# One ring for both caches of a decode attention, V in 64 KB rows, w_down on 64 partitions, all of wo last

## The chip, the cores and the metric

The kernel runs on one core of a Trainium2 chip. The metric is the device time of one execution in microseconds (us), the median of several runs. Five engines work side by side and are tied by semaphores: PE (matrix products), DVE (vector), ACT (activations), POOL, and SP, which here does nothing but issue the transfers (DMAs) from HBM to SBUF. SBUF has 128 partitions; PSUM is where PE accumulates.

## What is computed

Two branches of a decoding step for one token, mixed by a gate:

```python
q = (x @ wq).reshape(1, 1, 32, 128)               # x: 512, wq: 512 x 4096
scores = einsum("bhqd,bhkd->bhqk", q, k_cache) * 128 ** -0.5   # k_cache: 32 x 65536 x 128
o = einsum("bhqk,bhkd->bhqd", softmax(scores), v_cache)        # v_cache: 32 x 65536 x 128
a = o.reshape(1, 1, 4096) @ wo                    # wo: 4096 x 512
b = (silu(x @ w_gate) * (x @ w_up)) @ w_down      # 512 x 1792, 512 x 1792, 1792 x 512
g = sigmoid((x * gate_w).sum(-1))
out = g * a + (1 - g) * b
```

All is in bf16. The two caches are 537 MB each, and every byte of them is read once; all weights together are 14 MB.

## The kernel before

There are 32 heads of 65536 rows. A head is cut into G = 4 chunks of 16384 rows, so that K and V come in 128 chunks each, 4 MB a chunk: 128 rows of the cache (NB) in each of the 128 partitions, 32 KB in a row of HBM. A chunk n belongs to head n // 4.

For a chunk of K, `products` multiplies all rows by the head's query on DVE (line 228, one instruction in place) and halves the 128 products three times by additions (line 232); `scores` adds the remaining 16 columns up on PE with 16 products with the identity (line 242) into the head's 128x512 scores in PSUM. When a head's four chunks are in, `row_max` and `exponentials` take the largest score and write the weights P_sb; DVE does this between the halves of the next chunk's products. For a chunk of V, `values` issues 32 products of PE (line 290). At the end of a head, `head_copy` and `head_column` bring the four partial rows into a column oT (lines 303, 311, 318), and `project` multiplies it with the head's 128 rows of wo into a_ps (line 323). The feed-forward branch (`feed_forward_in`, `_mid`, `_out`) runs between the first chunks.

The schedule is manual: each engine does its instructions in the order in which the program writes them. Every transfer is issued by SP, in one queue, in the program's order, so a transfer whose place in SBUF is still in use holds up all that are issued after it. The large tiles come from one pool, `ring`, of SLOTS = 5 slots of 32 KB a partition: chunks of K, chunks of V, wq, w_gate with w_up, w_down and the second half of wo. A step of the main loop takes one chunk of K and one of V; V follows four chunks of K behind (up to eight later, `LAG` and `SPREAD`). The first half of wo comes in four pieces between the chunks into `wo_pool`, and the heads of that half are projected as they finish; the second half of wo is loaded after the last chunk of V, and its heads are projected at the end. Ahead of the main loop SP issues x, gate_w, wq, two chunks of K, w_gate, w_up, w_down and the first piece of wo.

The tile framework gives each transfer one of eight semaphores in turn, and adds a wait wherever an instruction touches bytes that an earlier one reads or writes, as far as it can tell from the two access patterns.

Of the kernel before, what the change touches and what calls it, by code (L numbers as in the profile page):

```python
# [11 lines left out]
P = 128  # L12
# [4 lines left out]
SLOTS = 5  # L17

WIDTH = 16

LAG = 8
SPREAD = 40
# [3 lines left out]
def kernel(  # L26
# [22 lines left out]
    FT = F // P  # L49
    G = Sk // (NB * P)  # L50
    NBH = Sk // P
    N = H * G
    QG = 4
    assert Dh == P and Sk % (NB * P) == 0 and NBH <= 512 and H % QG == 0 and G >= 2
# [3 lines left out]
    ring = ctx.enter_context(tc.tile_pool(name="ring", bufs=SLOTS))  # L58
    small = ctx.enter_context(tc.tile_pool(name="small", bufs=2))
    ppool = ctx.enter_context(tc.tile_pool(name="ppool", bufs=3))  # L60
    wo_pool = ctx.enter_context(tc.tile_pool(name="wo_pool", bufs=2))
# [7 lines left out]
    def big(name):  # L69
        return ring.tile([P, NB * Dh], bf16, name=name, tag="big")  # L70


    xT = consts.tile([P, KT], bf16, name="xT")
    gwT = consts.tile([P, KT], bf16, name="gwT")
    with nc.allow_non_contiguous_dma(reason="small"):
        nc.sync.dma_start(out=xT, in_=A_x[0, 0, :].rearrange("(p t) -> p t", t=KT))
        nc.sync.dma_start(out=gwT, in_=gate_w.rearrange("(p t) -> p t", t=KT))
    wq_t = big("wq_t")
    wq_sb = wq_t[:, : KT * H * Dh].rearrange("p (t f) -> p t f", t=KT)
    nc.sync.dma_start(out=wq_sb, in_=A_wq.rearrange("(p t) f -> p t f", t=KT))  # L80
# [9 lines left out]
    X_bc = consts.tile([P, KT, P], bf16, name="X_bc")  # L90
# [7 lines left out]
    b_sb = consts.tile([1, D], f32, name="b_sb")  # L98
    a_ps = psum_a.tile([1, D], f32, name="a_ps")

    K_tiles, V_tiles, S_tiles, P_tiles, O_tiles = {}, {}, {}, {}, {}

    def load(dst, cache, n, name, cuts=(0, NB)):
        h, g = divmod(n, G)
        t = big(name)
        view = t.rearrange("p (j d) -> p j d", d=Dh)
        src = cache[0, h, g * NB * P : (g + 1) * NB * P, :].rearrange("(p j) d -> p j d", j=NB)
        for a, b in zip(cuts[:-1], cuts[1:]):
            nc.sync.dma_start(out=view[:, a:b, :], in_=src[:, a:b, :])
        dst[n] = view  # L110

    load(K_tiles, A_k_cache, 0, "K_t")
    load(K_tiles, A_k_cache, 1, "K_t")

# [14 lines left out]
    for g in range(H // QG):  # L129
        queries(g)  # L130


    gu_t = big("gu_t")
    wgu_sb = gu_t[:, : 2 * KT * F].rearrange("p (w t f) -> p w t f", w=2, t=KT)
    nc.sync.dma_start(out=wgu_sb[:, 0], in_=B_w_gate.rearrange("(p t) f -> p t f", t=KT))
    nc.sync.dma_start(out=wgu_sb[:, 1], in_=B_w_up.rearrange("(p t) f -> p t f", t=KT))
    wd_t = big("wd_t")
    wd_sb = wd_t[:, : FT * D].rearrange("p (t n) -> p t n", t=FT)
    nc.sync.dma_start(out=wd_sb, in_=B_w_down.rearrange("(p t) n -> p t n", t=FT))
    WG = 4  # L140
    wo_tiles = {}

    WH = H // 2
    wo_end = []

    def load_wo_end(cuts):
        t = big("wo_t")[:, : (H - WH) * D].rearrange("p (h n) -> p h n", n=D)
        rows = A_wo[WH * P :, :].rearrange("(h p) n -> p h n", p=P)
        for a, b in zip(cuts[:-1], cuts[1:]):
            nc.sync.dma_start(out=t[:, a:b, :], in_=rows[:, a:b, :])  # L150
        wo_end.append(t)

    def load_wo(g):
        wo_tiles[g] = wo_pool.tile([P, WG, D], bf16, name="wo_sb")
        rows = A_wo[g * WG * P : (g + 1) * WG * P, :]
        nc.sync.dma_start(out=wo_tiles[g], in_=rows.rearrange("(h p) n -> p h n", p=P))

    load_wo(0)

    def feed_forward_in():  # L160

        gu_ps = psum_m.tile([P, 2 * FT], f32, name="gu_ps", tag="misc")
        for w in range(2):
            cols = wgu_sb[:, w].rearrange("p t (m c) -> p t c m", c=FT)
            for ft in range(FT):
                for t in range(KT):
                    nc.tensor.matmul(
                        gu_ps[:, w * FT + ft : w * FT + ft + 1],
                        lhsT=cols[:, t, ft, :],
                        rhs=xT[:, t : t + 1],  # L170
                        start=(t == 0),
                        stop=(t == KT - 1),
                    )
        gu_sb = consts.tile([P, 2 * FT], f32, name="gu_sb")
        nc.scalar.activation(out=gu_sb, in_=gu_ps, func=ACT.Copy)
        eg = consts.tile([P, FT], f32, name="eg")
        nc.scalar.activation(out=eg, in_=gu_sb[:, :FT], func=ACT.Exp, scale=-1.0)
        return gu_sb, eg

    def feed_forward_mid(gu_sb, eg):  # L180
# [10 lines left out]
        b_ps = psum_m.tile([1, D], f32, name="b_ps", tag="misc")  # L191
        for ft in range(FT):
            nc.tensor.matmul(  # L193
                b_ps,
                lhsT=hT[:, ft : ft + 1],
                rhs=wd_sb[:, ft, :],
                start=(ft == 0),
                stop=(ft == FT - 1),
            )
        g_ps = psum_m.tile([P, 1], f32, name="g_ps", tag="misc")  # L200
# [3 lines left out]
        return b_ps, eg2  # L204

    def feed_forward_out(b_ps, eg2):

# [5 lines left out]
        )  # L213
        nc.scalar.activation(out=b_sb, in_=b_ps, func=ACT.Copy, scale=rest)
        nc.tensor.matmul(a_ps, lhsT=ones_f[0:1, 0:1], rhs=b_sb, start=True, stop=False)  # L215


    def products(n, a=0, b=NB):

# [31 lines left out]
    def row_max(h):  # L251

        m = small.tile([P, 1], f32, name="m")
        nc.vector.tensor_reduce(out=m, in_=S_tiles[h], axis=AXIS.X, op=ALU.max)  # L254
        diag = small.tile([P, P], f32, name="diag")
# [17 lines left out]
    def total(h):  # L273

        tot_ps = psum_m.tile([P, 1], f32, name="tot_ps", tag="misc")
        nc.tensor.matmul(tot_ps, lhsT=ones_f, rhs=rowsum[:, h : h + 1], start=True, stop=True)  # L276
        return tot_ps
# [6 lines left out]
    def values(n):  # L284

        h, g = divmod(n, G)
        if g == 0:
            O_tiles[h] = psum_o.tile([4, 4 * Dh], f32, name="O_ps")
        for j in range(0, NB, 4):
            nc.tensor.matmul(  # L290
                O_tiles[h],
                lhsT=P_tiles[h][:, g * NB + j : g * NB + j + 4],
                rhs=V_tiles[n][:, j : j + 4, :],
                start=(g == 0 and j == 0),
                stop=(g == G - 1 and j == NB - 4),
            )
        del V_tiles[n]

    def head_copy(h, last=False):
        O_sb = small.tile([4, 4 * Dh], f32, name="O_sb")  # L300
# [21 lines left out]
    def project(h):  # L322
        nc.tensor.matmul(  # L323
            a_ps,
            lhsT=oT[:, h : h + 1],
            rhs=wo_tiles[h // WG][:, h % WG, :] if h < WH else wo_end[0][:, h - WH, :],
            start=False,
            stop=(h == H - 1),
        )


    steps = []
    v = 0
    for n in range(N):
        due = n >= G and not (n >= SPREAD and n % 4 == 3 and n - v < LAG)
        steps.append((n, v if due else None))
        v += due
    while v < N:
        steps.append((None, v))
        v += 1  # L340

    ff = done = tot_ps = None
    for n, v in steps:
        if n is not None and n > 1:
            load(K_tiles, A_k_cache, n, "K_t")
        if v is not None:
            if v % (WG * G) == 2 * G and v // (WG * G) + 1 < WH // WG:
                load_wo(v // (WG * G) + 1)
            load(V_tiles, A_v_cache, v, "V_t", (0, NB) if v < N - 2 else (0, 64, NB) if v < N - 1 else (0, 32, 64, 96, 112, NB))
            if v == N - 1:  # L350
                load_wo_end((0, 4, 8, 12, 14, 16))
        vector = iter(()) if n is None else products(n)
        top_of = None
        if n is None:
            top_of = H - 1 if S_tiles else None
        elif n % G == 0 and n > 0:
            top_of = n // G - 1
            vector = (i for a in (0, NB // 2) for i in products(n, a, a + NB // 2))
        if top_of is not None:
            next(vector, None)  # L360
            mT_ps = row_max(top_of)
            next(vector, None)
            exponentials(top_of, mT_ps)
        for _ in vector:
            pass
        if n == 1:
            ff = feed_forward_in()
        if n == 2:
            ff = feed_forward_mid(*ff)
        if n == 3:  # L370
            feed_forward_out(*ff)
        if tot_ps is not None:
            weight(*tot_ps)
            tot_ps = None
        if done is not None:
            head_column(done, head_copy(done))
        if v is not None:
            values(v)
        if top_of is not None:
            tot_ps = top_of, total(top_of)  # L380
        if n is not None:
            scores(n)
        if done is not None and done < WH:
            project(done)
        done = v // G if v is not None and v % G == G - 1 else None
    O_last = head_copy(H - 1, last=True)
    for h in range(WH, WH + 4):
        project(h)
    head_column(H - 1, O_last)
    for h in range(WH + 4, H):  # L390
        project(h)

    out_sb = consts.tile([1, D], bf16, name="out_sb")
# [32 lines left out]
```

## Time and profile before

| | |
|---|---|
| time, median of 3 runs | 2543.51 us (2541.84 to 2543.7) |
| profiled execution: time / span of the core | 2541.8 us / 2540.0 us |
| busy: PE / DVE / ACT | 1736.3 us (68%) / 2174.9 us (86%) / 75.7 us (3%) |
| read from HBM | 1087.64 MB, 428 GB/s over the span |
| mean clock granted to PE | 0.751 |

The profile's page is of one execution. "Busy" is the time in which an engine executes; the slices are 40 equal parts of the span, with a digit for tenths of busy time. The chain that ended last is followed back from the last instruction to what released it. The timeline lists instructions in the order of their start, with equal neighbours merged (xN), and in brackets the idle time before them and what ended it. A row with SPq is an issue of a transfer; the transfer itself lands later.

### The profile page before, as it was taken

The numbers are of one execution on the slowest core, as the hardware profiler recorded it, in microseconds if no ns is written. First come the engines' busy times: TensorE is split into PE (matmuls) and PEld (weight loads), VectorE is DVE, ScalarE is ACT, GpSimd is POOL, SyncE is SP. The second block draws the span as 40 slices with busy tenths as digits, with TensorE's granted clock in tenths as the row PEclk, the third lists the DMA queues.
The fourth block names the chain that finished last, engine by engine and source line by source line (L and its number), as shares of the span: only waits on it lengthen the run. The fifth ranks groups of instructions, "written<-read, shape, count | busy, mean of one in ns | idle before, by whom it ended". The sixth has DMA issues, their size and how long they took to land.

```text
span 2540.0 us, 15211 instructions
## 1 busy us (share of the span) xinstructions
PE 1736.3 (68%) x6722; PEld 707.9 (28%) x6722; DVE 2174.9 (86%) x780; ACT 75.7 (3%) x206; POOL 0.7 (0%) x6
## 2 busy tenths in 40 slices
PE   3577667776777656667776667677667776776679
PEld 2232222322223222222232223222222222222223
DVE  6999888888888999998888888888888888888860
ACT  1000000000000000000000000000000000000000
POOL 0000000000000000000000000000000000000000
PEclk7777776777777677777777777777777777777779
DMA  9999999999999999999999999999999999999998
GB/s 408 428 431 430 432 431 432 430 429 432 431 432 431 429 432 432 430 432 431 431 431 430 434 431 431 431 431 432 430 432 431 431 431 430 433 431 431 431 431 358
DMA packets 42755, 1088.61 MB, mean 429 GB/s; under 512 B 4673, under 2 KB 8770, under 8 KB 9026
## 3 DMA queue, kind: packets, MB, share of 16 engines
q1 hardware_dynamic: 42690, 1087.66, 99.7%
q8 instruction: 52, 0.85, 0.1%
q14 instruction: 13, 0.11, 0.0%
HBM read 1087.64 MB, written 0.00 MB: 428 GB/s over the span
## 4 chain that ended last, share of the span: by engine, by line
DMA 67%; PE 21%; DVE 11%; issue 1%; ACT 0%; SPq 0%; DVEq 0%
DMA V_t<-in_A_v_cache_dram 60%; PE O_ps L290 19%; DVE K_t L228 6%; DMA K_t<-in_A_k_cache_dram 5%; DVE K_t L232 5%; PE S_ps L242 1%; DMA wo_t<-in_A_wo_dram 1%; DMA wq_t<-in_A_wq_dram 0%; PE qg_ps L118 0%; PE oh_ps L311 0%; DVE m L254 0%; PE a_ps L323 0%; ACT P_sb L267 0%; PE a_ps L215 0%; DVE top L263 0%
## 5 line engine op out<-in xcount | busy, mean ns | idle before, releaser
L290 PE MATMUL O_ps<-V_t,P_sb 128*4 128x512 bf16 x4096 | 1159.0, 453 | 494.7 <-DMA V_t<-in_A_v_cache_dram 492.5
L228 DVE TENSOR_TENSOR K_t<-K_t,q_bc 128x16384 bf16<-128x16384 bf16 (+1 forms) x159 | 1117.2, 7026 | 267.5 <-DMA K_t<-in_A_k_cache_dram 259.1
L232 DVE TENSOR_TENSOR K_t<-K_t 128x2048 bf16<-128x2048 bf16 (+3 forms) x477 | 1030.5, 2160 | 14.2
L290 PEld LDWEIGHTS <-P_sb 128*4 128x4 bf16 x4096 | 394.2, 97 | 1240.9 <-issue 899.0
L242 PE MATMUL S_ps<-K_t,ident_b 128*128 128x128 bf16 x2048 | 464.4, 392 | 118.4 <-DVE K_t L232 118.4
L242 PEld LDWEIGHTS <-ident_b 128*128 128x128 bf16 x2048 | 225.6, 114 | 341.7 <-issue 148.3
L311 PE MATMUL oh_ps<-ident_f,O_sb 4*128 4x1 f32 x256 | 57.1, 340 | 73.7 <-ACT O_sb L303 73.7
L311 PEld LDWEIGHTS oh_ps<-ident_f,O_sb 4*128 4x128 f32 x256 | 54.4, 310 | 83.5 <-ACT O_sb L303 78.8
L256 ACT ACTIVATE diag<-ident_f,m 128x128 f32<-128x128 f32 x32 | 12.9, 402 | 2100.6 <-DVE m L254 2100.6
L258 PE MATMUL mT_ps<-diag,ones_f 128*128 128x128 f32 x64 | 24.0, 475 | 74.9 <-ACT diag L256 74.9
L305 DVE COPY O_sb<-O_ps 4x256 f32<-4x256 f32 x1 | 0.4, 412 | 52.7 <-ACT O_sb L303 52.7
L258 PEld LDWEIGHTS mT_ps<-diag,ones_f 128*128 128x128 f32 x64 | 14.9, 290 | 90.5 <-ACT diag L256 90.5
L254 DVE TENSOR_REDUCE m<-S_ps 128x1 f32<-128x512 f32 x32 | 21.9, 684 | 7.2 <-PE S_ps L242 7.2
L267 ACT ACTIVATE P_sb<-S_ps,bias 128x512 bf16<-128x512 f32 x32 | 22.0, 687 | 1.0
L303 ACT ACTIVATE O_sb<-O_ps 4x512 f32<-4x512 f32 (+1 forms) x32 | 18.1, 565 | 131.5 <-PE O_ps L290 131.5
L118 PE MATMUL qg_ps<-wq_t,X_bc 128*128 128x512 bf16 x32 | 9.6, 473 | 14.0 <-DMA wq_t<-in_A_wq_dram 14.0
L193 PE MATMUL b_ps<-wd_t,hT 128*1 128x512 bf16 x14 | 5.1, 545 | 15.7 <-DVE hT L186 15.7
L281 DVE RECIPROCAL recip<-tot_ps 128x1 f32<-128x1 f32 x32 | 5.1, 160 | 12.1 <-PE tot_ps L276 12.1
L276 PEld LDWEIGHTS tot_ps<-rowsum,ones_f 128*128 128x128 f32 x64 | 9.5, 188 | 14.0 <-issue 14.0
L276 PE MATMUL tot_ps<-rowsum,ones_f 128*128 128x1 f32 x64 | 12.2, 260 | 0.0
L318 ACT ACTIVATE oT<-oh_ps,rg 128x1 bf16<-128x1 f32 x32 | 8.4, 264 | 75.9 <-PE oh_ps L311 75.9
L263 DVE TENSOR_REDUCE top<-mT_ps 128x1 f32<-128x128 f32 x32 | 9.0, 283 | 1.2 <-PE mT_ps L258 1.2
(39 smaller groups left out, 64.6 us busy)
## 6 DMA issues: line engine op xcount, KB each, us to landing
K_t<-in_A_k_cache_dram SPq DMA_DIRECT2D x128, 4096.0 KB, 35.3
V_t<-in_A_v_cache_dram SPq DMA_DIRECT2D x126, 4096.0 KB, 29.5
wq_t<-in_A_wq_dram SPq DMA_DIRECT2D x1, 4096.0 KB, 12.3
V_t<-in_A_v_cache_dram SPq DMA_DIRECT2D x2, 2048.0 KB, 31.9
V_t<-in_A_v_cache_dram SPq DMA_DIRECT2D x3, 1024.0 KB, 31.1
wo_sb<-in_A_wo_dram SPq DMA_DIRECT2D x4, 512.0 KB, 36.9
gu_t<-in_B_w_gate_dram SPq DMA_DIRECT2D x1, 1792.0 KB, 34.6
gu_t<-in_B_w_up_dram SPq DMA_DIRECT2D x1, 1792.0 KB, 38.3
```

Of the source, the lines that this page charges most:

```text
L118: nc.tensor.matmul(qg_ps, lhsT=X_bc[:, t, :], rhs=wq_sb[:, t, g * QG * Dh : (g + 1) * QG * Dh], start=(t == 0), stop=(t == KT - 1),)
L228: yield nc.vector.tensor_tensor(out=K, in0=K, in1=q_rep, op=ALU.mult)
L232: yield nc.vector.tensor_tensor(out=K[:, :, 0:half], in0=K[:, :, 0:half], in1=K[:, :, half : 2 * half], op=ALU.add,)
L242: nc.tensor.matmul(S_tiles[h][:, g * NB : (g + 1) * NB], lhsT=ident_b, rhs=K_tiles[n][:, :, c], start=(c == 0), stop=(c == WIDTH - 1),)
L254: nc.vector.tensor_reduce(out=m, in_=S_tiles[h], axis=AXIS.X, op=ALU.max)
L256: nc.scalar.activation(out=diag, in_=ident_f, func=ACT.Copy, scale=m)
L258: nc.tensor.matmul(mT_ps, lhsT=ones_f, rhs=diag, start=True, stop=True)
L267: nc.scalar.activation(out=P_tiles[h], in_=S_tiles[h], func=ACT.Exp, bias=bias, scale=scale, accum_out=rowsum[:, h : h + 1],)
L276: nc.tensor.matmul(tot_ps, lhsT=ones_f, rhs=rowsum[:, h : h + 1], start=True, stop=True)
L290: nc.tensor.matmul(O_tiles[h], lhsT=P_tiles[h][:, g * NB + j : g * NB + j + 4], rhs=V_tiles[n][:, j : j + 4, :], start=(g == 0 and j == 0) ...
L303: nc.scalar.activation(out=O_sb[:, :cut], in_=O_ps[:, :cut], func=ACT.Copy)
L311: nc.tensor.matmul(oh_ps, lhsT=O_sb[:, c * Dh : (c + 1) * Dh], rhs=ident_f[0:4, c : c + 1], start=(c == 0), stop=(c == 3),)
```

## The change

All 192 KB of a partition that the ring takes are now one tensor of six units of 32 KB, and the program says which unit each load uses. Units 0 and 1, 2 and 3, 4 and 5 form pairs.

- K still comes in chunks of 4 MB, but the rows are dealt out so that a partition owns 256 rows of the cache in sequence (64 KB): a chunk of K reads the first or the second 32 KB of each such row. V comes in 64 loads of 8 MB, 64 KB a partition, into a pair of units (`load_v`); the last two of them are loaded in halves and smaller cuts.
- The main loop runs over pairs of K chunks: step j loads chunks 2j-1 and 2j into one pair of units and V load j-2 into the next, and uses V load j-2's first half in step j and its second in step j+1.
- w_down lies on 64 partitions, 28 rows of it in each (28 KB), in unit 4. It is loaded by eight transfers of eight partitions each, which are 4 partitions apart (`load_wd`): two before K chunk 2, two before chunk 3, two before chunk 4, two before the first V load. The hidden vector is brought into that layout by two products with columns of the identity (h_ps, h2), and its product with w_down takes 28 matmuls in place of 14, in `feed_forward_out`.
- SP's first load is the part of wq for heads 0 to 3, then x, K chunk 0, the rest of wq, gate_w, w_gate, w_up, K chunk 1. The products of K chunk 0 start after the first four heads' queries.
- wo is loaded whole after the last V, in seven cuts, and all 32 heads are projected at the end: 8 before the last head's column, 24 after.
- P_sb has two buffers instead of three; diag, O_sb and b_sb one.

The core of the diff:

```diff
-    ring = ctx.enter_context(tc.tile_pool(name="ring", bufs=SLOTS))
+    ring = consts.tile([P, UNITS * UNIT], bf16, name="ring")
+    def unit(u, size=UNIT, parts=P):
+        return ring[:parts, u * UNIT : u * UNIT + size]
+    def rows_of(cache, h, c):
+        rows = cache[0, h, c * 2 * NB * P : (c + 1) * 2 * NB * P, :]
+        return rows.rearrange("(p j) d -> p j d", j=2 * NB)
+    def load_k(n, u):
+        h, g = divmod(n, G)
+        view = unit(u).rearrange("p (j d) -> p j d", d=Dh)
+        half = g % 2
+        nc.sync.dma_start(
+            out=view, in_=rows_of(A_k_cache, h, g // 2)[:, half * NB : (half + 1) * NB, :]
+        )
+        K_tiles[n] = view
+    def load_v(w, pair):
+        h, c = divmod(w, 2)
+        view = ring[:, 2 * pair * UNIT : 2 * (pair + 1) * UNIT].rearrange("p (j d) -> p j d", d=Dh)
+        nc.sync.dma_start(out=view, in_=rows_of(A_v_cache, h, c))
...
+    nc.sync.dma_start(out=wq_sb[:, :, :first], in_=wq_rows[:, :, :first])
...
+    load_k(0, 1)
+    nc.sync.dma_start(out=wq_sb[:, :, first:], in_=wq_rows[:, :, first:])
...
+    wd_sb = unit(4, GT * D, HP).rearrange("p (t n) -> p t n", t=GT)
+    wd_rows = B_w_down.rearrange("(p t) n -> p t n", t=GT)
+    def load_wd(i):
+        lo = (0, 1, 2, 3, 32, 33, 34, 35)[i]
+        part = slice(lo, lo + 29, 4)
+        nc.sync.dma_start(out=wd_sb[part], in_=wd_rows[part])
...
-        for ft in range(FT):
-            nc.tensor.matmul(
-                b_ps,
-                lhsT=hT[:, ft : ft + 1],
-                rhs=wd_sb[:, ft, :],
...
+        h_ps = psum_m.tile([HP, GT], f32, name="h_ps", tag="misc")
+        for r in range(2):
+            nc.tensor.matmul(
+                h_ps[:, r * FT : (r + 1) * FT], lhsT=ident_b[:, r::2], rhs=hT, start=True, stop=True
+            )
+        h2 = consts.tile([HP, GT], bf16, name="h2")
+        nc.scalar.activation(out=h2, in_=h_ps, func=ACT.Copy)
...
+        for t in range(GT):
+            nc.tensor.matmul(
+                b_ps, lhsT=h2[:, t : t + 1], rhs=wd_sb[:, t, :], start=(t == 0), stop=(t == GT - 1)
+            )
...
+    queries(0)
+    drain(products(0))
+    for g in range(1, H // QG):
+        queries(g)
+    load_k(1, 3)
+    load_wd(0)
+    load_wd(1)
+    load_k(2, 5)
+    scores(0)
+    ff = feed_forward_in()
+    for j in range(1, last + 1):
+        a, b = 2 * j - 1, 2 * j
+        pair = 2 * (j - 2) % 3
+        if j == 2:
+            for i in range(3):
+                load_wd(2 + 2 * i)
+                load_wd(3 + 2 * i)
+                if i < 2:
+                    load_k(3 + i, i)
+        elif j > 2:
+            load_k(a, 2 * pair)
+            load_k(b, 2 * pair + 1)
+        if j == last:
+            load_k(NK - 1, 2 * ((pair + 1) % 3))
+        elif j >= 2:
+            load_v(j - 2, (pair + 1) % 3)
+        drain(products(a))
+        if j == 1:
+            ff = feed_forward_mid(*ff)
...
+        if j >= 3:
+            values(j - 3, 1)
...
+        if j == last:
+            load_v(j - 2, (pair + 2) % 3)
+        scores(a)
...
+        if b % G == 0:
+            sums = maximum(b // G - 1, (i for c in (0, NB // 2) for i in products(b, c, c + NB // 2)))
+        else:
+            drain(products(b))
...
+        if j == 2:
+            feed_forward_out(*ff)
+        if j >= 2:
+            values(j - 2, 0)
+        scores(b)
+    drain(products(NK - 1))
+    values(NV - 3, 1)
+    O_sb = head_copy(H - 2)
+    load_v_half(NV - 2, 0, 2 * pair)
+    load_v_half(NV - 2, 1, 2 * pair + 1)
+    load_v_half(NV - 1, 0, 2 * spare + 1, (0, 64, NB))
+    scores(NK - 1)
+    head_column(H - 2, O_sb)
+    weight(*maximum(H - 1, iter(())))
+    load_v_half(NV - 1, 1, 2 * spare, (0, 32, 64, 96, 112, NB))
...
+    cuts = (0, 8, 16, 22, 26, 29, 31, 32)
+    for lo, hi in zip(cuts[:-1], cuts[1:]):
+        nc.sync.dma_start(out=wo_sb[:, lo:hi, :], in_=wo_rows[:, lo:hi, :])
+    for w in (NV - 2, NV - 1):
+        for half in range(2):
+            values(w, half)
+    O_sb = head_copy(H - 1, last=True)
+    for h in range(8):
+        project(h)
+    head_column(H - 1, O_sb)
+    for h in range(8, H):
+        project(h)
```

## Prediction

> **What bounds the kernel now.** I read the slices first, then the chain, then the timeline at both ends.
>
> ```profile
> span 2540.0 us, 15211 instructions
> ...
> DVE  6999888888888999998888888888888888888860
> ...
> DMA  9999999999999999999999999999999999999998
> GB/s 408 428 431 430 432 431 432 430 429 432 431 432 431 429 432 432 430 432 431 431 431 430 434 431 431 431 431 432 430 432 431 431 431 430 433 431 431 431 431 358
> ...
> DMA 67%; PE 21%; DVE 11%; issue 1%; ACT 0%; SPq 0%; DVEq 0%
> ```
>
> The transfers are the bound: 431 GB/s from the second slice to the 39th, and no engine is full. Only the outer slices (63.5 us each) fall short, by (431-408)/431 x 63.5 = 3.4 us and (431-358)/431 x 63.5 = 10.8 us. At 431 GB/s a 4 MB chunk takes 9.73 us. So what matters is whether SP keeps the queue fed, and what is left to do when the last bytes land. The timeline of the start:
>
> ```profile
> 1.66 0.42 SPq L80 DMA_DIRECT2D wq_t<-in_A_wq_dram  x1
> 2.13 0.91 SPq L109 DMA_DIRECT2D K_t<-in_A_k_cache_dram  x2
> ...
> 57.20 3.63 PE L242 MATMUL S_ps<-K_t,ident_b 128*128 128x128 bf16 x16 [6.35 <-DVE K_t L232]
> 58.95 8.69 DVE L228 TENSOR_TENSOR K_t<-K_t,q_bc 128x16384 bf16<-128x16384 bf16 x1 [1.81 <-DMA K_t<-in_A_k_cache_dram]
> ...
> 67.68 8.01 DVE L232 TENSOR_TENSOR K_t<-K_t 128x8192 bf16<-128x8192 bf16 x3
> ```
>
> By 5.1 us SP has issued 18.6 MB, so DVE's 16.7 us a chunk (8.69 + 8.01) hides behind transfers. And the end:
>
> ```profile
> 2461.33 3.63 PE L242 MATMUL S_ps<-K_t,ident_b 128*128 128x128 bf16 x16
> ...
> 2466.24 0.64 PE L258 MATMUL mT_ps<-diag,ones_f 128*128 128x128 f32 x2 [1.29 <-ACT diag L256]
> ...
> 2468.78 1.86 PE L311 MATMUL oh_ps<-ident_f,O_sb 4*128 4x1 f32 x8 [1.90 <-ACT O_sb L303]
> ...
> 2470.57 8.38 PE L290 MATMUL O_ps<-V_t,P_sb 128*4 128x512 bf16 x32
> ...
> 2479.20 20.88 PE L290 MATMUL O_ps<-V_t,P_sb 128*4 128x512 bf16 x96
> ...
> 2534.19 2.94 PE L323 MATMUL a_ps<-wo_t,oT 128*1 128x512 bf16 x12
> ```
>
> A chunk of V costs PE 8.4 to 9.9 us after idling, 7.0 when it runs on (20.88/3); a projection 0.245. The last matmul ends at 2537.1, 2.9 us before the span.
>
> **The start: what the slices of w_down wait for.** A slice of eight partitions, 4 apart, spans in the flat addresses of `ring` whole partitions, all six units. The framework therefore orders it against every unit. The changed program's SP queue, with what each row waits for, decoded from its semaphore counts:
>
> ```
> K1          -
> w_down 0,1  K1 landed, w_gate/w_up landed, products(0)
> K2          w_down 0,1 landed, queries done
> w_down 2,3  products(2) and scores(2) done
> K3          w_down 2,3 landed
> w_down 4,5  K3 landed
> K4          w_down 4,5 landed
> w_down 6,7  K4 landed
> V0          w_down 6,7 landed
> K5          all 28 w_down matmuls done
> ```
>
> But for the last row, these waits are not needed by the data: unit 4 is free from the start. products(1) and scores(0) wait for w_down 0,1 in the same way, products(3) for 6,7. Behind each such row stands the whole queue, and nothing covers the wait, for all that was issued has landed.
>
> Prices: a K chunk on an empty queue takes 12.3 us from issue to landing (wq's row, same size and shape). A small transfer takes 1.8 (xT's row). A w_down row of 28 KB takes 28/32 of the 1.215 us that one 32 KB packet has in the trace's DMA records, 1.06; no transfer here has eight rows. Side by side in eight engines, a pair costs 1.8 + 2 x 1.06 = 3.9; one row after another, 1.8 + 17 = 18.8. I take 3.9, as every 128-row load here is spread over sixteen, and keep 18.8 for a rival. The Trainium skill, DMA: Bandwidth & Descriptors, section on why a DMA increments its semaphore by 16, says that a transfer uses the largest number of engines up to 16 that divides its slowest dimension: eight here; by it the pair costs 3.9, and no run here shows one yet.
>
> The walk, in us from the span's start. w_up lands at 42.0 before, with wq, K0, K1 and w_gate. K1 takes that place; the first large load is issued 0.9 earlier, and wq in short rows costs 0.5 more: K1 at 41.6. w_down 0,1: 45.5. products(1): 62.2; feed_forward_mid (1.05): 63.2; products(2): 79.9; scores(2): 83.6. From K2's landing (57.8) to here nothing moves. Then 3.9, 12.3, 3.9, 12.3, 3.9 in a row: w_down 2,3 at 87.6, K3 99.9, 4,5 at 103.8, K4 116.1, 6,7 at 120.0. products(3): 136.7, scores(3): 140.4, largest score and weights (4.2, as at 100.05 to 104.2 before) and total: 145.0. 28 matmuls: 5.1 for the 14 of line 193 and 3.0 for 14 more at the settled rate: 153.1 (157 if they stay at 0.43). V0 landed at 142. K5 is issued at 153.1 and lands at 165.4, K6 at 175.1.
>
> Before, the landing records put K6 at 117.2, with the same 8 MB of V and with w_down and 0.5 MB of wo. So the start loses **57.9**, and 1.5 more for that piece of wo, which now comes later.
>
> **The middle.** From K6 on, a step is 16 MB, 38.9 us. A V load may start when scores of the chunk in its pair's second unit are done, and these stand on PE behind the previous V load's first half. From the V's landing: 9.9 + 3.6 + 0.3 of issue + 2.6 until bytes flow (wq: 12.3 less 9.7) = 16.4. Behind that V two chunks of K are queued, 19.5 us. The cover is 3.1, so I count zero; DVE's 34 us in 38.9 end sooner.
>
> Fewer, longer rows: the records give 1,215 ns for 32 KB and 613 for 16 KB, so joining two packets saves 11 ns. 62 V loads, 8 packets an engine: 62 x 8 x 11 ns = **-5.5**; if a 64 KB row is sent as two, 0.
>
> K's rows now lie 64 KB apart instead of 32. No row shows the effect; I take none. The same page of the skill, section on latency and other measured facts, speaks against it: copies of 16 KB rows ran at 207 instead of 214 GB/s with rows 512 KB apart, and slower at larger steps. It lists nothing as close as 64 KB. By 207/214 the 2490 us of cache loads would grow by 84.
>
> **The end.** V load 61 must land before its first half, the scores of chunk 126, its second half and the scores of 127 can follow on PE: 9.3 + 3.6 + 7.0 + 3.6 = 23.5. To the next V product 4.5 (5.6 before, less an O_sb copy that is done earlier). Then the four last halves, 8.4 + 20.9 = 29.3, then 8 projections, the column, 24 projections: 2.0 + 1.05 + 5.9 = 9.0. In all 66.3 from that landing. The transfers behind it are four chunks (38.9) and wo (12.2, twice the 6.1 that the last 2 MB take): 51.1, or 57 with the second half of load 62, which waits for the scores of 126. So wo is hidden behind PE and the end goes by PE: 66.3 - 51.1 = **+15.2**. If PE's weights and products overlap better, +8; if each first chunk is slow, +18. After the last matmul 2.9 remain, against 3.5 between last landing and end before: -0.6.
>
> **Sum.** 2540.0 + 57.9 + 1.5 - 5.5 + 15.2 - 0.6 = 2608.5. The profiled execution lies 1.8 above its span, and the median 1.7 above that execution: 2612. Everything else hides under the transfers: diag, O_sb, b_sb in one buffer, two P_sb, the two h_ps matmuls.
>
> **Rivals.**
> - *w_down's eight rows go one after another*: four pairs at 18.8 instead of 3.9, +60: 2672. Nothing in the trace excludes it. 0.08.
> - *The ring is too tight in the middle*: it decides once a V half takes over 13 us. The page's mean of 453 ns a product x 32 is 14.5, which would cost 1.5 in each of 60 steps: 2700. The timeline's runs of 8.4 to 9.9 speak against it. 0.10.
> - *The wider step between rows slows the caches*: 1% is +25, 3% is +75: 2640 to 2690. 0.05.
> - *Not slower: the w_down waits don't bite*, since the rows count as issued without holding SP, and the queue stays fed. Then the start gives -0.9 + 0.5 - 4.3 (w_down off half of the engines; the sixteen parts of a load land 0.3 us apart at the start and 10.9 at the end, eight of them late) = -4.7, and with an end hidden by an earlier PE: 2540 - 4.7 + 1.5 - 5.5 - 0.6 = 2530.7, 2534 as a time. It decides when start and end together lose less than 4.6. Before, SP's waits for PE and DMA hold it for hundreds of us, which speaks against it. 0.05.
>
> **How the numbers follow.** The forecast has 0.72. Its bounds: pair of w_down 2.9 to 5.5, -4 to +6; 64 KB rows, +5.5; the end, -7 to +3; 28 matmuls, +4; the ring's cover, a few us. That gives 2601 to 2631. I widen it to 2597, as these may add up with terms that I count at zero, and to 2642 for the light cases of the third rival; the first two and the fourth lie outside. A change under 0.2% (5 us) can't be told from none here. Faster 0.03 and same 0.02 are the last rival, with its end hidden or partly exposed; slower 0.95.
>
> **What would show it.** Right: the second slice near 190 GB/s, the first and third near 320 and 340; SP waiting some 38 us for the scores at the third w_down slice; DVE's third K chunk ending near 80 and its sixth starting near 165; about 431 to 433 GB/s in the middle; PE busy for some 9 us after the last wo lands. Wrong: the first slices above 400 GB/s, a middle below 425, or V waiting for K's scores on SP in every step with the transfers idle.

## The result and the profile after

The changed kernel takes 2619.69 us (median of 4 runs, 2618.05 to 2621.14) against 2543.35 us for the kernel before on the same chip. The ratio is 1.030, with a 95% interval of 1.0288 to 1.0313: slower by 76 us. The forecast was 2612 in a range of 2597 to 2642. The profiled execution has a span of 2619.4 us, where the working of the prediction came to 2608.5.

The page of the changed kernel, of the same rows as before:

```profile
span 2619.4 us, 15068 instructions
...
DVE  5378988898898898898898898888888889889891
...
DMA  7479999999999999999999999999999999999997
GB/s 320 195 307 431 425 437 432 428 435 433 430 434 434 427 433 436 421 434 435 430 431 433 431 429 437 432 427 437 431 427 432 431 432 432 432 428 432 438 425 273
...
DMA 64%; PE 33%; DVE 2%; SPq 0%; issue 0%; ACT 0%; DVEq 0%
...
L212 PE MATMUL b_ps<-ring,h 64*1 64x512 bf16 x28 | 12.1, 625 | 0.0
```

All of the loss lies in the first three slices and the last one. A slice is now 65.5 us; below 431 GB/s the first three lose 16.9, 35.9 and 18.8 us, and the last one 24.0. Before, the first lost 3.4 and the last 10.8. Between them the queue runs at 431 as before. The 28 matmuls of w_down take 12.1 us: one starts every 0.43 us, and they overlap, which is why a single one counts 625 ns.

What SP waited for, by line (total, number of times, longest):

```profile
SPq L87 <- PE b_ps L212: 37.5, 1, 37.5
SPq L128 <- DVE ring L240: 34.1, 1, 34.1
SPq L128 <- DMA ring<-in_A_k_cache_dram: 33.1, 3, 11.8
SPq L128 <- DMA ring<-in_B_w_up_dram: 27.1, 1, 27.1
...
SPq L87 <- DMA ring<-in_B_w_down_dram: 10.2, 3, 3.5
```

Line 128 is the issue of a slice of w_down, line 87 that of a chunk of K. The slices wait for the products of a chunk, for chunks of K, and for w_up. None of these touches a byte of w_down's place. The first row is the true wait: chunk K5 goes to that place, so it has to wait for the w_down matmuls. V load 0, issued ahead of it, lands at 145.9, so the transfers stand still for the last 16 of these 37.5 us. The first 162 us, from the timeline:

```profile
42.48 1.50 SPq L128 DMA_DIRECT2D ring<-in_B_w_down_dram  x2
...
47.30 8.69 DVE L236 TENSOR_TENSOR ring<-ring,q_bc 128x16384 bf16<-128x16384 bf16 x1 [15.32 <-DMA ring<-in_B_w_down_dram]
...
47.35 0.34 SPq L87 DMA_DIRECT2D ring<-in_A_k_cache_dram  x1
...
85.46 1.32 SPq L128 DMA_DIRECT2D ring<-in_B_w_down_dram  x2
90.28 0.33 SPq L87 DMA_DIRECT2D ring<-in_A_k_cache_dram  x1
...
119.28 1.32 SPq L128 DMA_DIRECT2D ring<-in_B_w_down_dram  x2
...
124.08 8.69 DVE L236 TENSOR_TENSOR ring<-ring,q_bc 128x16384 bf16<-128x16384 bf16 x1 [42.35 <-DMA ring<-in_B_w_down_dram]
...
149.77 12.10 PE L212 MATMUL b_ps<-ring,h 64*1 64x512 bf16 x28
...
161.91 0.80 SPq L87 DMA_DIRECT2D ring<-in_A_k_cache_dram  x2
```

This is the walk of the prediction, row by row. DVE stands still for 15.3 and for 42.4 us, and both times w_down's landing ends it. Issue and landing alternate, a pair of slices (4.8 to 4.9 us until the next row goes out) and a chunk (12.0 to 12.2 us), with nothing queued behind. K5 goes out at 161.9 when the last w_down matmul ends. Its products start at 174.1, and K6, a chunk later, lands at 183.7; before it was 117.2. Landings like these are from the trace's records of when the sixteen parts of a transfer report. And the end:

```profile
2549.17 10.02 PE L297 MATMUL O_ps<-ring,P_sb 128*4 128x512 bf16 x32 [18.38 <-DMA ring<-in_A_v_cache_dram]
...
2559.12 3.64 PE L250 MATMUL S_ps<-ring,ident_b 128*128 128x128 bf16 x16
2562.69 8.40 PE L297 MATMUL O_ps<-ring,P_sb 128*4 128x512 bf16 x32
...
2579.02 29.48 PE L297 MATMUL O_ps<-ring,P_sb 128*4 128x512 bf16 x128
...
2611.14 5.34 PE L329 MATMUL a_ps<-ring,oT 128*1 128x512 bf16 x24
```

PE idles 18.4 us for V load 61, and from then on runs almost without a break for 67.3 us.

### The profile page after: what moved, and what is told of

Read it like the earlier page. It is cut to its first block, busy times and chain, and to the rows that moved or that the text cites. A ratio compares the mean times of both kernels' runs of the same rounds, so it can differ in the third digit from the quotient of the medians.

```text
span 2619.4 us, 15068 instructions
## 1 busy us (share of the span) xinstructions
PE 1641.3 (63%) x6738; PEld 708.8 (27%) x6738; DVE 2170.9 (83%) x780; ACT 75.5 (3%) x207; POOL 0.7 (0%) x6
## 4 chain that ended last, share of the span: by engine, by line
DMA 64%; PE 33%; DVE 2%; SPq 0%; issue 0%; ACT 0%; DVEq 0%
DMA ring<-in_A_v_cache_dram 61%; PE O_ps L297 23%; PE S_ps L250 9%; DMA ring<-in_A_k_cache_dram 2%; DVE ring L236 1%; DVE ring L240 1%; DMA ring<-in_B_w_down_dram 1%; PE b_ps L212 0%; PE a_ps L329 0%; SPq L128 0%; PE oh_ps L317 0%; PE a_ps L223 0%; ACT P_sb L274 0%; PE tot_ps L282 0%; PE mT_ps L265 0%
## 5 line engine op out<-in xcount | busy, mean ns | idle before, releaser
L236 DVE TENSOR_TENSOR ring<-ring,q_bc 128x16384 bf16<-128x16384 bf16 (+1 forms) x159 | 1116.7, 7023 | 371.9 <-DMA ring<-in_A_k_cache_dram 314.2
L297 PE MATMUL O_ps<-ring,P_sb 128*4 128x512 bf16 x4096 | 1045.5, 420 | 378.5 <-DMA ring<-in_A_v_cache_dram 378.5
L240 DVE TENSOR_TENSOR ring<-ring 128x2048 bf16<-128x2048 bf16 (+3 forms) x477 | 1030.3, 2160 | 14.2
L250 PE MATMUL S_ps<-ring,ident_b 128*128 128x128 bf16 x2048 | 465.7, 394 | 495.6 <-DVE ring L240 481.1
L297 PEld LDWEIGHTS <-P_sb 128*4 128x4 bf16 x4096 | 370.3, 92 | 1035.9 <-issue 623.8
L250 PEld LDWEIGHTS <-ident_b 128*128 128x128 bf16 x2048 | 234.1, 117 | 725.1 <-issue 549.5
L282 PE MATMUL tot_ps<-rowsum,ones_f 128*128 128x1 f32 x64 | 18.8, 363 | 49.1 <-ACT P_sb L274 49.1
L282 PEld LDWEIGHTS tot_ps<-rowsum,ones_f 128*128 128x128 f32 x64 | 16.1, 312 | 58.5 <-ACT P_sb L274 58.5
L153 PE MATMUL qg_ps<-ring 128*128 128x512 bf16 x32 | 10.6, 505 | 22.2 <-DMA ring<-in_A_wq_dram 17.0
L212 PE MATMUL b_ps<-ring,h 64*1 64x512 bf16 x28 | 12.1, 625 | 0.0
## 6 DMA issues: line engine op xcount, KB each, us to landing
ring<-in_A_v_cache_dram SPq DMA_DIRECT2D x2, 4096.0 KB, 12.1
```

Of the source, the lines that this page charges most:

```text
L153: nc.tensor.matmul(qg_ps, lhsT=X_bc[:, t, :], rhs=wq_sb[:, t, g * QG * Dh : (g + 1) * QG * Dh], start=(t == 0), stop=(t == KT - 1),)
L236: yield nc.vector.tensor_tensor(out=K, in0=K, in1=q_rep, op=ALU.mult)
L240: yield nc.vector.tensor_tensor(out=K[:, :, 0:half], in0=K[:, :, 0:half], in1=K[:, :, half : 2 * half], op=ALU.add,)
L250: nc.tensor.matmul(S_tiles[h][:, g * NB : (g + 1) * NB], lhsT=ident_b, rhs=K_tiles[n][:, :, c], start=(c == 0), stop=(c == WIDTH - 1),)
L297: nc.tensor.matmul(O_tiles[h], lhsT=P_tiles[h][:, col + j : col + j + 4], rhs=V[:, j : j + 4, :], start=(col == 0 and j == 0), stop=(col = ...
```

## The experiments

The times below are medians. The kernel before took 2542.6 to 2543.0 beside them. Versions 1 to 4 each build on the one ahead, and "the repaired version" is version 5.

**1. w_down in one load.** If the slices' waits cost the start, taking the slices away must give most of it back.

```diff
-    def load_wd(i):
-        lo = (0, 1, 2, 3, 32, 33, 34, 35)[i]
-        part = slice(lo, lo + 29, 4)
-        nc.sync.dma_start(out=wd_sb[part], in_=wd_rows[part])
+    def load_wd():
+        nc.sync.dma_start(out=wd_sb, in_=wd_rows)
...
-    load_wd(0)
-    load_wd(1)
+    load_wd()
...
-            for i in range(3):
-                load_wd(2 + 2 * i)
-                load_wd(3 + 2 * i)
-                if i < 2:
-                    load_k(3 + i, i)
+            for i in range(2):
+                load_k(3 + i, i)
```

> The changed kernel with w_down's eight slices replaced by one load of the same 64 partitions, all at once, with K3, K4 and the first V behind it in the old order. A load of partitions 0 to 63 covers unit 4 alone, so nothing else in the ring is ordered against it; the only wait left at the start is a true one: the load into unit 4 (chunk K5) waits for the 28 w_down matmuls, which stand behind the products of chunk 4 on DVE. Theory (the start is lost to the slices' waits): the second chunk's products no longer idle for w_down, K5 is issued near 120 us instead of 161.9 and K6 lands near 136 instead of 184.2; the middle and the end are as they were: about 2572, 48 us under the changed kernel, still some 28 over the kernel before. Rival (the ring's shared units or the row step, not the slices, starve the queue): the slow slices at the start stay, 2610 to 2620.

Measured: 2574.28, that is 45.4 less. Its timeline:

```profile
31.80 4.04 SPq L87 DMA_DIRECT2D ring<-in_A_k_cache_dram  x3
...
46.01 8.69 DVE L234 TENSOR_TENSOR ring<-ring,q_bc 128x16384 bf16<-128x16384 bf16 x1 [14.23 <-DMA ring<-in_A_k_cache_dram]
...
106.32 12.10 PE L210 MATMUL b_ps<-ring,h 64*1 64x512 bf16 x28
...
118.45 0.80 SPq L87 DMA_DIRECT2D ring<-in_A_k_cache_dram  x2
```

K2, K3 and K4 go out together at 31.8, no engine waits for w_down, K5 goes out at 118.5. The slices' waits are the largest part of the loss. One thing was not foreseen: the 64 rows of this one load took 2.23 us each (median of the DMA records), though in the eight-partition slices of version 7 each row of 28 KB takes 1.06. So the load took twice the 4.3 us that it took on 128 partitions. The Trainium skill, SBUF — State Buffer, section Door 1, on the DMA port swizzle, says that a transfer's rate goes by how many of sixteen ports its partitions reach, and by its table partitions 0 to 63 reach eight of them: half the rate. The records agree, and the expectation had not weighed it.

**2. The w_down matmuls a step earlier.**

```diff
-    def feed_forward_out(h2, eg2):
+    def feed_forward_down(h2, eg2):
...
+        b_sb = wide.tile([1, D], f32, name="b_sb", tag="wide")
+        nc.scalar.activation(out=b_sb, in_=b_ps, func=ACT.Copy)
+        return b_sb, eg2
+
+    def feed_forward_out(b_sb, eg2):
...
-        nc.tensor.matmul(a_ps, lhsT=ones_f[0:1, 0:1], rhs=b_sb, start=True, stop=False)
+        nc.tensor.matmul(a_ps, lhsT=rest, rhs=b_sb, start=True, stop=False)
...
+        if j == 1:
+            ff = feed_forward_down(*ff)
```

> The one-load version, with the 28 w_down matmuls moved from behind the products of chunk 4 to the end of the step before (their result is copied to SBUF unscaled, and the scale by the gate goes into the weight of the one-row matmul that adds it). K5 then waits for nothing that is late. Theory (what is left of the start's loss is the wait of K5 for those matmuls): K6 lands near 116 us, and the time is 18 to 22 us under the one-load version, about 2551. Rival (K5's wait is hidden behind the V load queued ahead of it): within 3 us of the one-load version.

Measured: 2567.15, 7.1 less and not 18 to 22. K6 does land 19 us earlier (121.3 instead of 140.1), but V load 1 lands only 9.7 earlier (151.1 instead of 160.8):

```profile
116.10 8.38 PE L298 MATMUL O_ps<-ring,P_sb 128*4 128x512 bf16 x32
...
124.41 3.64 PE L251 MATMUL S_ps<-ring,ident_b 128*128 128x128 bf16 x16
...
128.08 0.33 SPq L95 DMA_DIRECT2D ring<-in_A_v_cache_dram  x1
...
151.15 9.61 PE L298 MATMUL O_ps<-ring,P_sb 128*4 128x512 bf16 x32 [12.53 <-DMA ring<-in_A_v_cache_dram]
```

V load 1 goes into the pair of K3 and K4. It waits for the scores of K4, which stand on PE behind V0's first half, and are late because DVE works off four chunks at 16.7 us each from K1's late landing on. It is issued at 128.1, 6.8 us after the last chunk ahead of it had landed. Taking one wait away uncovered the next.

**3. PE's order at the end.**

```diff
+        if j == last:
+            scores(b)
         if j >= 2:
             values(j - 2, 0)
-        scores(b)
+        if j < last:
+            scores(b)
...
     drain(products(NK - 1))
-    values(NV - 3, 1)
...
     scores(NK - 1)
+    mT_ps = row_max(H - 1)
+    exponentials(H - 1, mT_ps)
+    values(NV - 3, 1)
```

> The version before with PE's order at the end changed: in the last step the scores of chunk 126 stand ahead of the first half of V load 61, and the scores of 127, the largest score and the exponentials ahead of its second half. Theory (the end goes by PE's chain from the landing of V load 61, and two stretches of scores and the 4.5 us of the last head's weights stand in it): the chain falls from 67 to about 60 us after that landing, since this work is then done before it, and the second half of V load 62 is no longer late; 6 to 7 us faster, about 2544. Rival (the end goes by the transfers behind V load 61, 51 us of them): 10 us or more faster or, if the chain waits for the half that lands last anyway, within 2 us.

Measured: 2564.92, 2.2 less. PE's chain from V61's landing to the last matmul is 61.2 us where version 2 has 66.3, as expected; but V61 landed 3.7 us later in the profiled execution, 2.2 of that already at V load 1. So the size of the chain is confirmed, and the gain in time is not.

**4. V in rows of 32 KB.**

```diff
-        nc.sync.dma_start(out=view, in_=rows_of(A_v_cache, h, c))
+        rows = rows_of(A_v_cache, h, c)
+        for a, b in ((0, NB), (NB, 2 * NB)):
+            nc.sync.dma_start(out=view[:, a:b, :], in_=rows[:, a:b, :])
```

> The version with the reordered end, with each 8 MB load of V issued as two loads of 32 KB rows, into the same units and under the same waits. Theory (a 64 KB row goes as one packet and saves the fixed part of one; 2421 ns against 2 x 1215 in the records): 62 loads x 8 packets an engine x 9.5 ns = 4.7 us slower than the version with 64 KB rows, some 0.2%. Rival (the queue is limited by the memory or by the engines that fetch instructions, so packet size counts for nothing): within 1 us.

Measured: 2561.88, 3.0 faster, where both theories said slower or equal. The edit changes two things: the rows, and also when a load may start. The first half of V1 now needs only K3's unit: it goes out at 101.1 instead of 129.8, the second half lands at 144.3 and not at 153.4. That is a gain of 9.1 us at the start, more than the rows cost. The two had to be told apart (6).

**5. A repaired version.**

```diff
     load_k(0, 1)
+    load_k(1, 3)
     nc.sync.dma_start(out=wq_sb[:, :, first:], in_=wq_rows[:, :, first:])
...
-    wd_sb = unit(4, GT * D, HP).rearrange("p (t n) -> p t n", t=GT)
-    wd_rows = B_w_down.rearrange("(p t) n -> p t n", t=GT)
+    wd_sb = unit(4, FT * D).rearrange("p (t n) -> p t n", t=FT)
+    wd_rows = B_w_down.rearrange("(p t) n -> p t n", t=FT)
...
-            load_v(j - 2, (pair + 1) % 3)
+            if j < 4:
+                v_halves(j - 2, (pair + 1) % 3)
+            else:
+                load_v(j - 2, (pair + 1) % 3)
...
-            load_v(j - 2, (pair + 2) % 3)
+            v_halves(j - 2, (pair + 2) % 3)
```

> The version with the reordered end, with four repairs that the runs so far point to: w_down on 128 partitions as before (its one load of 64 partitions took 2.24 us a row instead of 1.06, 4.4 us too long), K1 queued ahead of the rest of wq, and V loads 0, 1 and 61 in two halves each; with its second half there earlier, V61's products stand ahead of the scores of 127 again. The other 59 V loads keep 64 KB rows. Theory (what was still lost: some 5 us up to K6's landing, 12 us while V load 1 waits for the scores of chunk 4, and PE's chain of 61 us behind V61's landing, where 51 us of transfers stand): K6 lands near 117, no gap before V1, the chain from V61's last bytes falls to about 55; 2540 to 2545, that is the kernel before within 2 to 3 us. Rival (the ring itself, with V pairs that wait for K's scores, costs time in the middle): not under 2555.

Measured: 2547.63, 72 us under the changed kernel and 0.19% over the one before (interval 0.11% to 0.28%). The start is whole again: K6 lands at 115.8 and V1 at 135.2, right behind it. The rival falls. The estimate of 2540 to 2545 was 3 too low at its upper end: the chain from the last bytes of V61 is 60 us, not 55, because PE takes up V61 only at 2479.0, after the scores of 126, though its first half was in at 2471:

```profile
2478.97 15.88 PE L296 MATMUL O_ps<-ring,P_sb 128*4 128x512 bf16 x64
```

**6. Rows of 32 KB, nothing else.**

```diff
-            if j < 4:
-                v_halves(j - 2, (pair + 1) % 3)
-            else:
-                load_v(j - 2, (pair + 1) % 3)
+            v_halves(j - 2, (pair + 1) % 3)
```

> The repaired version with the other 59 V loads in halves too, so that start and end are the same and only rows of 32 KB stand for rows of 64 KB in the middle. Theory (a V load of 64 KB rows has a period of 19.34 us, two chunks of 32 KB rows have 2 x 9.71): 59 x 0.08 = 4.7 us slower than the repaired version. Rival (the earlier run with 32 KB rows was faster because of its rows, and not because its V1 could start before both units were free): 3 us faster.

Measured: 2552.82, 5.2 slower than the repaired version; expected were 4.7. The row of packets on the two pages, 64 KB rows first:

```profile
DMA packets 35138, 1088.60 MB, mean 428 GB/s; under 512 B 3713, under 2 KB 8322, under 8 KB 9090
```

```profile
DMA packets 43635, 1088.61 MB, mean 427 GB/s; under 512 B 4657, under 2 KB 9266, under 8 KB 10034
```

A packet of 64 KB takes 2421 ns and two of 32 KB 2 x 1215, so the larger rows are worth 9 ns a packet. This part of the change is a gain.

**7. Eight slices in three tensors, and 8. the same in one.** Version 7 is the repaired version with w_down in eight slices again and the ring in three tensors. Version 8 is version 7 with one tensor:

```diff
-    ring = [consts.tile([P, 2 * UNIT], bf16, name=f"ring{i}") for i in range(UNITS // 2)]
+    ring = consts.tile([P, UNITS * UNIT], bf16, name="ring")
...
-        lo = u % 2 * UNIT
-        return ring[u // 2][:parts, lo : lo + size]
+        return ring[:parts, u * UNIT : u * UNIT + size]
...
-        view = ring[pair].rearrange("p (j d) -> p j d", d=Dh)
+        view = ring[:, 2 * pair * UNIT : 2 * (pair + 1) * UNIT].rearrange("p (j d) -> p j d", d=Dh)
```

> The repaired version with w_down again as the change has it, 64 partitions in eight slices and 28 matmuls, but the ring is three tensors of one pair each instead of one tensor, the broadcast of x lies outside it, and the slices are issued in between the first loads. In addition the scores of 126 stand between the two halves of V61 on PE. Theory (a slice is ordered against everything in its tensor, so in a tensor of its own pair it meets only K2, which needs not be early): no wait of note at the start, K2 lands near 58 and K6 near 117; the end is 2.5 us shorter, since PE now begins V61 when it lands; w_down on half the engines gives 0 to 4: 2540 to 2546. Rival (eight-partition slices are slow by themselves): K6 after 122, 2550 or more.

> The three-tensor version with the ring as one tensor again and nothing else changed: the same instructions in the same order, only the waits differ. Theory (it is the one flat tensor that makes the slices wait): slices 0 and 1 wait for K0, K1 for them, slices 2 and 3 for K1, w_gate for slices 2 to 5, slices 6 and 7 for w_gate, w_up for them; with 4.9 us for a pair and 12.3 for a chunk on an empty queue K1 lands near 32 and K2 near 76 instead of 58: 18 us slower than the version with three tensors (14 to 22). Rival (what holds the queue are the slices and not their waits): within 3 us.

Measured: 2548.65 in three tensors, 2583.03 in one. The same instructions in the same order differ by 34.4 us through waits alone. So it is neither the slices nor the 64 partitions, but the one flat tensor. The size was under-estimated, 18 for 34, because only SP's side was counted: K2 lands at 78.7 instead of 60.9 in version 7, the 18 us of the expectation. The other side is what DVE waits for. Version 8:

```profile
14.98 1.47 SPq L124 DMA_DIRECT2D ring<-in_B_w_down_dram  x2
19.95 0.33 SPq L87 DMA_DIRECT2D ring<-in_A_k_cache_dram  x1
...
61.54 0.33 SPq L139 DMA_DIRECT2D ring<-in_B_w_up_dram  x1
61.70 8.69 DVE L248 TENSOR_TENSOR ring<-ring,q_bc 128x16384 bf16<-128x16384 bf16 x1 [56.24 <-DMA ring<-in_B_w_down_dram]
```

In version 7 the same products start when the chunk has landed:

```profile
15.12 8.69 DVE L249 TENSOR_TENSOR ring<-ring,q_bc 128x16384 bf16<-128x16384 bf16 x1 [9.66 <-DMA ring<-in_A_k_cache_dram]
```

The very first products, of a chunk that lies in SBUF from 15 us on, wait in version 8 until 61.7 for the last slices. DVE is still 35 us late at the fourth chunk, and V1 lands 35 late with it. Version 7 missed its range (2540 to 2546) by 2.7, without reaching its rival's mark: K6 lands at 119.9 and not after 122, and all 64 rows of the slices take 1.06. It has no gain over the repaired version (+1.0): its slices cost 3.5 us at the start (K2's products at 60.95 instead of 57.42) and 4.1 up to K6, while V61's first half starts on PE when it lands, which gave 1.8 back. Between the two profiled executions that is 3.1 us; the repaired version's was among its fastest.

**9. The old end on the repaired version.** V61 in one load, and PE's order as in the changed kernel.

```diff
-            v_halves(j - 2, (pair + 2) % 3)
+            load_v(j - 2, (pair + 2) % 3)
...
-        if j == last:
-            scores(b)
         if j >= 2:
             values(j - 2, 0)
-        if j < last:
-            scores(b)
+        scores(b)
```

> The repaired version with the end as the changed kernel has it: V61 in one load of 64 KB rows, its first half ahead of the scores of 126, its second half ahead of the scores of 127. Start and middle are the repaired version's. Theory (the end is PE's chain behind V61's landing: 67.3 us in the changed kernel, 60.1 from the last bytes of V61 in the repaired version): 7 us slower than the repaired version, about 2555. Rival (the transfers set the end in both): within 2 us.

Measured: 2550.89, 3.3 slower than the repaired version: less than the 7 of the theory, more than the 2 of the rival. V61's landing to the last matmul takes 64.6 us here (2481.99 to 2546.5), not 67.3, since the two halves of V61 ran in 8.63 and 7.07 us and not in 10.02 and 8.40:

```profile
2481.99 8.63 PE L296 MATMUL O_ps<-ring,P_sb 128*4 128x512 bf16 x32 [18.38 <-DMA ring<-in_A_v_cache_dram]
...
2494.13 7.07 PE L296 MATMUL O_ps<-ring,P_sb 128*4 128x512 bf16 x32
```

The order of PE's work and the load of V61 are worth some 3 us; the same 32 products, which take from 7.07 to 10.02 us in these rows, can make as much.

**10. w_down on 64 partitions in the kernel before,** eight slices in a tile of their own, so that nothing waits for them.

```diff
+    HP = P // 2
+    GT = F // HP
+    wd_sb = wd_t[:HP, : GT * D].rearrange("p (t n) -> p t n", t=GT)
+    slices = [slice(lo, lo + 29, 4) for lo in (0, 1, 2, 3, 32, 33, 34, 35)]
...
+    load_wd(0, 2)
     nc.sync.dma_start(out=wgu_sb[:, 0], in_=B_w_gate.rearrange("(p t) f -> p t f", t=KT))
+    load_wd(2, 4)
```

> The kernel before with w_down alone on 64 partitions, in the eight slices of the change, in a tile of its own, so that nothing waits for it; its 28 matmuls and the two that lay out h are the changed kernel's. Theory (w_down's rows go to eight of sixteen engines, and before eight of sixteen parts of every load land up to 10.9 us late at the end): if the eight rows go to the early engines, 64 rows x 1.06 us over 8 engines (8.5 us) instead of 4.3 on all, so 4 us faster, about 2539. First rival: they go to the late ones, 4 us slower, 2547. Second rival: slices that overlap on the same partitions are held up as the one load of 64 partitions was (2.24 us a row instead of 1.06), up to 4 us slower.

Measured: 2540.43, a ratio of 0.9991 (0.9982 to 1.0): 2.2 us less, where the interval goes from 4.6 less to none, so a gain is not shown, and both rivals with their 4 us more fall. The rows of the slices took 1.06 us each. The second slice of its span loses 8 us, the later ones make it up:

```profile
GB/s 409 373 434 432 431 435 430 434 432 431 434 432 433 432 433 433 432 432 434 432 432 434 432 434 431 433 432 433 433 431 435 431 434 432 434 433 431 434 431 363
```

It is the only version that did not end above the kernel before.

## Why the prediction was right, and where it was short

- **The start** was named with its mechanism: false waits of the slices, each with the whole queue behind it. Versions 1 and 8 show it from both sides. Its size was 57.9; K6's landing says 183.7 - 117.2 = 66.5. Of these, 43.6 go with the slices (K6 at 140.1 in version 1), 18.8 with the wait of K5 for the matmuls (121.3 in version 2), and the 4.1 by which version 2 is still later than the kernel before are about what its one load of 64 partitions takes too long. Three terms of the sum were short. A pair of slices until the next row is issued: 3.9 against 4.8 to 4.9 measured, 3.8 in all for four. The two slices of a pair use the same eight engines one after the other, as assumed; but the first rows take 1.2 to 1.9 us, the later ones 1.06 to 1.27, and the two issues alone hold SP for 1.3 to 1.5. The 28 matmuls: 8.1 against 12.1, the upper end that was kept for the range; all 28 ran at 0.43 us. The first slice, at K1's landing: 41.6 against 42.5, 0.9.
- **"The rows count as issued without holding SP"**, the rival on the other side, is excluded by SP's 34.1 us at line 128.
- **w_down's eight rows one after another** (pairs of 18.8) is excluded too: the pairs took 4.9.
- **The middle** was put at no loss, and -5.5 for the longer rows. From K6's landing to V61's it took 2365 us in the changed kernel, 2365 in the repaired version and 2371 in version 6 with its rows of 32 KB. The kernel before took 2374, with 1.5 MB of wo in between, which at 431 GB/s are some 4 us. So the tight ring never decided, and the rows brought what was said.
- **The wider step of K's rows** cost nothing: a 32 KB packet takes 1215 ns before and after. The rule of the Trainium skill that was weighed against it (DMA: Bandwidth & Descriptors, Latency and other measured facts) lists no step as small as this one, and by the records it does not reach down to 64 KB.
- **The end** was put at 66.3 us from V61's landing and took 67.3. Errors of both signs are in it: the two halves of V61 took 10.0 and 8.4 instead of 9.3 and 7.0, the projections and the column 8.1 instead of 9.0.
- **The step from span to time** helped by luck. The working put the span at 2608.5, and it was 2619.4, 10.9 more. The forecast in time is only 7.7 short, because 3.5 was added for a median above the profiled span, and this time the profiled execution was the longest of four, so that the median lies 0.3 above its span.
- **The signs that were named** came: 195 GB/s in the second slice, SP waiting 34.1 + 3.7 us for products and scores at the third slice of w_down, DVE's third chunk ending at 81.7, some 431 in the middle, PE busy for 8.7 us after the last of wo lands. The sixth chunk on DVE began at 174.1 and not near 165, by the same 8.7 us that the start was short.

With the start, the rows and the end as measured, the sum is 2540.0 + 66.5 + 1.5 - 5.2 + 16.2 - 0.6 = 2618.4, against a span of 2619.4. The 16.2 is 67.3 less the 51.1 of transfers that the prediction put behind V61, and the 1.5 is its estimate too. Version 9 checks it in another way. It has the changed kernel's middle and end but a whole start, and lies 68.8 us under it, 70.2 between the profiled executions: K6 lands at 115.9, 67.8 earlier, and the chain at the end is 2.7 shorter, 70.5 together. And it lies 7.9 over the kernel before: the end 13.5 (16.2 less those 2.7), the piece of wo 1.5, the rows -5.2, K6 -1.3, the last step -0.6, which makes 7.9.

The start had more layers than the slices' waits. The next one, K5's wait for the late w_down matmuls, is in the prediction's table; the one behind it, V1's wait for the scores of K4, is not. With both other waits gone, in version 2, V1 lands 29.8 us after K6, against 19.4 in the repaired version: 10 us. Its reason is that K1 stands behind 7 MB of weights in the queue, so that DVE idles 14 us before its second chunk (14.23 in version 1). It made no difference to the number, since the larger waits covered it.

## What to carry to other kernels

A partition-strided slice of a large tensor can be ordered against everything in that tensor, in both directions: the load waits for the neighbours, and their readers wait for the load. Count both sides from the semaphores, or give what is sliced a tensor of its own. When a wait is removed, work out at once what is late next on the same queue, because the gain is only the difference to that. And a coarser load saves a little on each packet but moves two moments: it starts only when all of its space is free and ends only when all of it is in, which counted here at both ends of the stream and not in its middle.

## What the runs showed of the hardware that was not expected

- A load of 64 neighbouring partitions ran at half the rate of one of 128: 2.23 us for a row of 28 KB, against 1.06 in eight-partition slices and 0.535 for 14 KB on 128 partitions.
- A row of 64 KB goes as one packet of 2421 ns: 9 ns less than two of 32 KB, 5.2 us over 59 loads.
- The sixteen parts of a load drift apart with small V loads and not with large ones. At the end of the stream they land 10 to 11 us apart before and in version 6, seven of them early and nine late, but 3.5 to 5 in the changed kernel and in the repaired version, which differs from version 6 in V's loads alone. A whole V load is issued only some 5 us ahead of its first bytes' turn, so an early part has to wait there; that this is the cause was argued and not tried. It cost no time that could be seen.
